# Attention and feed-forward on one Trainium2 core: when token loads, transposes and scores are issued

## The chip, the cores and the metric

The kernel runs on one core of a Trainium2 chip. Times are device microseconds (us). A run of one core has one time; I quote medians and say how many runs they are of. A profile shows one execution: its span goes from the first to the last instruction, and the time of that execution lies about 2 us above it. PE is TensorE, DVE VectorE, ACT ScalarE, POOL GpSimd and SP SyncE. PE multiplies; ACT and DVE empty its PSUM banks; POOL scales softmax rows, reorders tokens and issues the loads that cast to bf16; SP issues the DMA transposes and the output stores, in its program order.

## The reference, cut to what matters

```python
def _attn_ref(x, state):            # x (8, 8, 512, 64), state (8, 8, 32, 64)
    scale = 1.0 / np.sqrt(D)
    a = softmax(scale * x @ state.T)        # tokens read from the state
    xread = a @ state
    a2 = softmax(scale * state @ x.T)       # the state reads from the tokens
    sread = a2 @ x
    return np.concatenate([xread, sread], axis=2)

def _moe_ref(x, w1, w2, w3, w_out):         # 4352 rows of 512, d_ff 768
    h = np.maximum(np.maximum(x @ w1, x @ w2), x @ w3)
    return h @ w_out
```

(The softmax lines are abridged.) For each of eight batches the kernel folds `state @ w` into small matrices M, so that the up-projections of a batch are `M.T @ a.T`. They need the attention matrix transposed (`aT`); the scores need the tokens transposed (`xT`).

## The kernel before: the parts that matter

The program is written as strings of units, worked off in order. An opening handles batches 0 to 2, then one PERIOD string runs per batch and LAST ends it.

```python
PERIOD = """
u u u L u u S u S X o o u u P o o m M m u R u o o u m M m u u u u u u o u o
"""
...
    def load_x(b):                              # L: POOL issues the load, with a cast
        x_sb[b] = xlp.tile([128, H, J, D], BF16, tag="x", name="x")
        nc.gpsimd.dma_start(out=x_sb[b]..., in_=x[b]...)
...
            elif what == "S":
                scores(nb, sc.pop(0), "g")      # exp on ACT, sum on DVE, product a on POOL
            elif what == "P":
                if nb + 1 < B:
                    permute_x(nb + 1, None, "g")    # POOL: xn <- x
                    x_crossbar(nb + 1)              # SP: DMA transpose xT <- xn
            elif what == "L":
                if nb + 1 < B:
                    load_x(nb + 1)
            elif what == "X":
                a_crossbar(nb)                      # SP: DMA transpose aT <- a
```

In period t, `nb` is t + 2: that batch is scored, while the up-projections (`u`) of batch t + 1 and the output rows (`o`) of batch t run. The last rows of all:

```python
        if last and j == J - 1:
            half = d_model // 2
            for k in range(2):
                o = res.tile([128, half], F32, name=f"oh{k}")
                f = slice(k * half, k * half + half)
                copy("av"[k], o, po[:, f])          # ACT, then DVE, out of one bank
                (nc.scalar, nc.sync)[k].dma_start(out=rows[j][:, f], in_=o)
```

The softmax here doesn't subtract the row's maximum and nothing guards it: scores larger than these inputs give would overflow.

Of the kernel before, what the change touches and what calls it, by code (L numbers as in the profile page):

```python
# [8 lines left out]
F32 = mybir.dt.float32  # L9
# [16 lines left out]


OPENING = """
id, idle 9, sel, idle 9, pm 0 0 a, lx 1, pm 0 1 v, pm 1 0 v, lw 0 1, xT 0 0 a, lw 2 4,
pm 1 1 v, xT 0 1 a, lw 1 2, S 0 0 g, S 0 1 g, xT 1 0 a, xT 1 1 v, M 0 0 aa, M 1 0 av,  # L30
R 0, lw 4 6, S 1 1 g, lx 2, S 1 0 g, aT 0 0 a, idle 7, aT 0 1 a, M 0 3 aa, M 0 2 aa,
M 1 2 va, R 1, u 0 0 0, u 0 3 0, M 0 1 va, u 0 0 1, u 0 3 1, u 0 2 0, aT 1 - v, M 1 3 aa,
u 0 1 0, u 0 3 2, u 0 0 2, lx 3, u 0 1 1, M 0 5 aa, M 0 4 va, u 1 2 0, u 0 2 1, lo,
pm 2 - g, u 1 0 0, u 1 2 1, pm 3 - g, M 2 5 av, M 1 5 av, u 0 1 2, u 0 5 0, xb 3,
u 0 4 0, u 0 2 2, u 1 3 0, xT 2 0 a, u 0 5 1, u 0 5 2, M 1 4 aa, M 1 1 aa, u 0 4 1,
xT 2 1 v, u 1 2 2, u 1 0 1, u 0 4 2, S 2 0 g, u 1 3 1, u 1 1 0, u 1 5 0, S 2 1 g,
u 1 4 0, o 0 0 0 v, o 0 0 1 a, o 0 1 0 a, u 1 0 2, o 0 1 1 a, u 1 5 1, M 2 2 aa, ab 2,
M 2 3 aa, M 2 0 av, o 0 2 0 a, u 1 4 1, o 0 2 1 a, u 1 3 2, M 2 4 aa, M 2 1 aa, u 1 5 2,
u 1 1 1, R 2, o 0 3 0 v, o 0 3 1 a, u 1 1 2, u 1 4 2
"""  # L40


PERIOD = """
u u u L u u S u S X o o u u P o o m M m u R u o o u m M m u u u u u u o u o
"""
LAST = """
u u M M u u P u u u L S u R o S u u M X u u o M u u u M u u o M u o o o o o
"""


# [1 line left out]
def kernel(  # L52
# [14 lines left out]
    nc = tc.nc  # L67

    B, H, S, D = x.shape
    _, _, Ns, _ = state.shape  # L70
    HD = H * D
    SP = S + Ns
    d_model, d_ff = moe_w1.shape
    assert HD == d_model and D == 64 and Ns == 32 and H == 8 and S == 512
    J = S // 128
    HP = H // 2
    MT = d_ff // 128
# [6 lines left out]
    res = ctx.enter_context(tc.tile_pool(name="res", bufs=1))  # L84
# [9 lines left out]
    def bank(shape, dt, name):  # L94
        return psum.tile(shape, dt, tag="bank", name=name)
# [3 lines left out]
    def copy(eng, o, i):  # L99
        if eng == "a":  # L100
            nc.scalar.copy(out=o, in_=i)  # L101
        else:
            ENG[eng].tensor_copy(out=o, in_=i)  # L103

    def mm(out_ap, lhsT, rhs, start, stop, pos=(0, 0)):
        nc.tensor.matmul(out_ap, lhsT, rhs, start=start, stop=stop, tile_position=pos)  # L106

    def tr(out_ap, in_ap):
# [9 lines left out]
        out=st32.rearrange("p n d -> p (n d)"),  # L118
        in_=state.rearrange("b h (q n) d -> (b h q) (n d)", q=2))
# [3 lines left out]
                      in_=x[0].rearrange("h (p j) d -> p h (j d)", j=J))  # L123
# [12 lines left out]
    wout = res.tile([128, MT, d_model], BF16, name="wout")  # L136
# [14 lines left out]
    def load_x(b):  # L151
        x_sb[b] = xlp.tile([128, H, J, D], BF16, tag="x", name="x")
        nc.gpsimd.dma_start(
            out=x_sb[b].rearrange("p h j d -> p h (j d)"),
            in_=x[b].rearrange("h (p j) d -> p h (j d)", j=J))
# [23 lines left out]
    def m_unit(b, m, engs):  # L179
        pm = [bank([128, 512], F32, "pm") for _ in range(2)]  # L180
        for hp in range(HP):
            for par in range(2):
                r0 = par * 64
                mm(pm[par][hp * 32:(hp + 1) * 32, 0:384],
                   sbd[r0:r0 + 64, b, hp, par, :],
                   W[r0:r0 + 64, :, hp, m * 128:(m + 1) * 128],
                   True, True, pos=(r0, hp * 32))
        for par in range(2):
            copy(engs[par], M_sb[:, b, m, par].rearrange("p i f -> p (i f)"), pm[par][:, 0:384])


    tiles = {}
# [21 lines left out]
    def permute_x(b, h, eng):  # L214
        j = slice(0, J) if h is None else slice(2 * h, 2 * h + 2)
        i = x_sb[b][:, :, j] if b else x32[:, :, j]
        copy(eng, x_nat(b)[:, j], i.rearrange("p h j d -> p j h d"))

    def x_crossbar(b):
        nc.sync.dma_start_transpose(  # L220
            out=xT(b).rearrange("p j hp t -> p (j hp) t"),
            in_=x_nat(b).rearrange("p j h d -> p (j h d)"))
# [27 lines left out]
    def a_crossbar(b):  # L250
        nc.sync.dma_start_transpose(
            out=aT(b).rearrange("p j a t -> p (j a) t"),
            in_=a_of(b).rearrange("p j a hp n -> p (j a hp n)"))
# [32 lines left out]
    def up(g, m, i):  # L286

        nn = S if g < B else ST
        ht = tile_of("ht", g, htp, [128, MT, S])
        pw = bank([128, S], F32, "pw")  # L290
        if g < B:
            for par in range(2):
                mm(pw, M_sb[:, g, m, par, i, :], aT(g)[:, :, par, :], par == 0, par == 1)
        else:
            for hp in range(HP):
                mm(pw[:, :nn], W[:, i, hp, m * 128:(m + 1) * 128], AT[:, hp, :],
                   hp == 0, hp == HP - 1)
        if i == 0:
            t = tiles["t", g, m] = tmpp.tile([128, S], BF16, tag="t0", name="t0")
            nc.scalar.copy(out=t[:, :nn], in_=pw[:, :nn])  # L300
        elif i == 1:
            t0 = tiles["t", g, m]
            t = tiles["t", g, m] = tmpp.tile([128, S], BF16, tag="t1", name="t1")
            nc.vector.tensor_max(t[:, :nn], t0[:, :nn], pw[:, :nn])  # L304
        else:
            nc.vector.tensor_max(ht[:, m, :nn], tiles["t", g, m][:, :nn], pw[:, :nn])  # L306

    def out_half(g, j, h, eng):
        last = g == ORDER[-1]
        if h == 0:  # L310
            tiles["po"] = bank([128, d_model], F32, "po")
        po = tiles["po"]
        for kt in range(3 * h, 3 * h + 3):
            mm(po, tiles["ht", g][:, kt, j * 128:(j + 1) * 128], wout[:, kt, :],
               kt == 0, kt == MT - 1)
        if h == 0:
            return
        rows = out[g * SP:g * SP + S, :].rearrange("(p j) f -> j p f", j=J) if g < B else None
        if last and j == J - 1:
            half = d_model // 2  # L320
            for k in range(2):
                o = res.tile([128, half], F32, name=f"oh{k}")
                f = slice(k * half, k * half + half)
                copy("av"[k], o, po[:, f])
                (nc.scalar, nc.sync)[k].dma_start(out=rows[j][:, f], in_=o)
            return
        if j % 2 == 0:
            tiles["o"] = op.tile([128, 2, d_model], F32, tag="o", name="o")
        o = tiles["o"]
        copy(eng, o[:, j % 2, :], po)  # L330
        if last:
            nc.sync.dma_start(out=rows[j], in_=o[:, j % 2, :])
        elif g < B:
            if j % 2 == 1:
                nc.sync.dma_start(out=rows[j - 1:j + 1].rearrange("j p f -> p j f"), in_=o)
        else:
            for q in range(4):
                bb = 4 * j + q
                nc.sync.dma_start(out=out[bb * SP + S:(bb + 1) * SP, :],
                                  in_=o[q * 32:(q + 1) * 32, j % 2, :])  # L340
# [46 lines left out]
    for t in range(1, B):  # L387
        p, g = ORDER[t], ORDER[t + 1]
        nb = t + 2
        us = [(g, m, i) for m in range(MT) for i in range(3)]  # L390
        os = [(p, j, h) for j in range(J if p < B else ST // 128) for h in range(2)]
        sc = [0, 1]
        for what in (PERIOD if g != ORDER[-1] else LAST).split():
            if what == "u":
                up(*us.pop(0))
            elif what == "o":
                if os:
                    out_half(*os.pop(0), "a")
            elif what in ("M", "m"):
                if m_q:  # L400
                    m_unit(*m_q.pop(0), "aa" if what == "M" else "av")
            elif nb >= B:
                continue
            elif what == "S":
                scores(nb, sc.pop(0), "g")
            elif what == "P":
                if nb + 1 < B:
                    permute_x(nb + 1, None, "g")
                    x_crossbar(nb + 1)
            elif what == "L":  # L410
                if nb + 1 < B:
                    load_x(nb + 1)
            elif what == "R":
                state_reads(nb)
            elif what == "X":
                a_crossbar(nb)
    for j in range(J):
        for h in range(2):
            out_half(ORDER[-1], j, h, "a")
# [29 lines left out]
```

## Time and profile before

| | before |
|---|---|
| first timed runs | 170.55 us median of 3 (167.83 to 172.34) |
| the profiled execution | 165.97 us, span 163.9 us |
| PE busy | 151.4 us, 92% of the span |
| next busiest | DVE 68%, ACT 57% |
| PE idle after 17 us and before its end | 5.5 us in four holes |

PE sets the time, and the holes in its work are what can be gained; the prediction shows both. What it describes in words is the order in two queues. These are lines of the order of work in the kernel before, first of POOL's queue, then of SP's (start, length, engine, line, operation):

```profile
71.89 1.04 POOL L246 TENSOR_TENSOR a<-e,rden 128x512 bf16<-128x512 bf16 x1 [0.46 <-DVE rden L245]
72.88 1.89 POOL L103 COPY xn<-x 128x2048 bf16<-128x2048 bf16 x1
74.71 0.94 POOL L153 DMA_DIRECT2D x<-in_x_dram  x1
...
72.96 1.24 SPq L251 DMA_TRANSPOSE aT<-a  x1
74.79 2.52 SPq L220 DMA_TRANSPOSE xT<-xn  x1
```

POOL reorders one batch's tokens as soon as its softmax products are done, and then at once issues the next load (74.71). The end of the same reordering releases the token transpose on SP (74.79). The two start within 0.1 us of each other, in every period that has a load.

### The profile page before, as it was taken

Reading aid. Unit: us, or ns where it says so; the run is one execution under the profiler, and the core shown is the slowest. Engines: PE = TensorE matmul, PEld = TensorE weight load, DVE = VectorE, ACT = ScalarE, POOL = GpSimd, SP = SyncE. Lnnn points to the kernel's source line nnn. Section 1 sums busy time; section 2 is a strip of 40 time slices with the busy share of each in tenths; the row PEclk is TensorE's granted clock in tenths of the full one; section 3 lists DMA queues with packets and bytes.
Section 4 is the critical chain, followed back from the end, with each engine's and each line's share of the span. In section 5 each row is a group of like instructions: output and inputs, shape, how many; then the busy total and the mean of one; then the engine's idle time right before and its main releaser. Section 6 shows DMA issues by size and latency. Waiting matters only on the chain. (4 is left out here: it accounts for less than half of the span.)

```text
span 163.9 us, 3537 instructions
## 1 busy us (share of the span) xinstructions
PE 151.4 (92%) x1389; PEld 74.7 (46%) x1389; DVE 112.0 (68%) x203; ACT 93.5 (57%) x184; POOL 44.6 (27%) x48
## 2 busy tenths in 40 slices
PE   7979999999929999799969999999999999999990
PEld 2455544554405444344424444454544476844430
DVE  3349999886836888578957797789778942558601
ACT  3688869776515665556545764576656534344340
POOL 8838944425000830074004600450050000000000
PEclk9999999999999999999999999999999999999999
DMA  5999999943990099907991899156306031130263
GB/s 166 286 185 196 187 198 201 159 101 79 154 194 24 4 161 112 285 18 119 116 287 57 87 173 285 42 117 203 134 0 192 0 132 65 63 128 0 68 192 130
DMA packets 35457, 21.73 MB, mean 133 GB/s; under 512 B 20592, under 2 KB 32880, under 8 KB 35440
## 3 DMA queue, kind: packets, MB, share of 16 engines
q1 hardware_dynamic: 20896, 14.55, 36.9%
q0 software_dynamic: 14400, 6.82, 35.9%
q8 instruction: 11, 0.18, 0.5%
q10 hardware_dynamic: 144, 0.13, 0.2%
q14 instruction: 6, 0.05, 0.1%
HBM read 15.20 MB, written 8.91 MB: 147 GB/s over the span
## 5 line engine op out<-in xcount | busy, mean ns | idle before, releaser
L106 PE MATMUL pw<-aT,M_sb 128*128 128x512 bf16 x288 | 72.2, 380 | 3.0 <-DMA aT<-a 3.0
L106 PE MATMUL po<-wout,ht 128*128 128x512 bf16 x204 | 50.4, 379 | 0.0
L304 DVE TENSOR_TENSOR t<-t,pw 128x512 bf16<-128x512 bf16 (+1 forms) x54 | 35.0, 650 | 20.7 <-ACT t L300 11.1
L106 PEld LDWEIGHTS <-M_sb 128*128 128x128 bf16 x288 | 25.7, 98 | 35.2 <-issue 4.8
L300 ACT CAST t<-pw 128x512 bf16<-128x512 f32 (+1 forms) x54 | 30.4, 572 | 18.8 <-PE pw L106 17.8
L306 DVE TENSOR_TENSOR ht<-t,pw 128x512 bf16<-128x512 bf16 (+1 forms) x54 | 34.9, 650 | 6.1 <-PE pw L106 3.4
L101 ACT COPY o<-po 128x512 f32<-128x512 f32 x33 | 19.3, 586 | 34.4 <-PE po L106 34.2
L246 POOL TENSOR_TENSOR a<-e,rden 128x512 bf16<-128x512 bf16 x16 | 16.6, 1041 | 69.3 <-ACT e L238 45.7
L101 ACT CAST M_sb<-pm 128x384 bf16<-128x384 f32 x69 | 28.4, 498 | 2.0 <-PE pm L106 1.3
L106 PEld LDWEIGHTS <-ht 128*128 128x128 bf16 x204 | 19.5, 98 | 21.8 <-issue 0.3
L103 DVE CAST M_sb<-pm 128x384 bf16<-128x384 f32 x27 | 14.0, 551 | 3.5 <-PE pm L106 3.5
L242 DVE TENSOR_REDUCE den<-e 128x16 f32<-128x512 bf16 x16 | 10.8, 672 | 3.5 <-ACT e L238 3.3
L103 POOL COPY xn<-x 128x2048 bf16<-128x2048 bf16 x6 | 11.4, 1892 | 4.8 <-DMA x<-in_x_dram 4.8
L238 ACT ACTIVATE e<-ps 128x512 bf16<-128x512 f32 x16 | 9.5, 599 | 5.3 <-PE ps L106 5.0
L106 PE MATMUL pm<-W,sbd 64*32 64x384 bf16 x384 | 11.8, 327 | 0.0
L106 PE MATMUL ps<-sbd,xT 128*128 128x64 bf16 x128 | 6.2, 193 | 4.1 <-DMA xT<-xn 2.6
L144 POOL DMA_DIRECT2D W<-in_moe_w_dram x12 | 9.0, 773 | 2.7 <-DMA x<-in_x_dram 2.7
L106 PE MATMUL pz<-zeros 128*128 128x512 bf16 x25 | 8.2, 486 | 1.2 <-DVE zeros L125 1.2
L106 PEld LDWEIGHTS <-xT 128*128 128x128 bf16 x128 | 5.3, 98 | 8.2 <-DMA xT<-xn 4.0
L106 PE MATMUL pw<-AT,W 128*128 128x256 bf16 x72 | 8.7, 273 | 0.0
L106 PEld LDWEIGHTS <-W 128*128 128x128 bf16 x72 | 7.0, 98 | 1.9
L279 DVE RECIPROCAL rd<-pr 128x128 f32<-128x128 f32 x8 | 7.6, 955 | 0.0
(38 smaller groups left out, 66.1 us busy)
## 6 DMA issues: line engine op xcount, KB each, us to landing
out_dram<-o SPq DMA_DIRECT2D x14, 512.0 KB, 4.1
x<-in_x_dram POOLq DMA_DIRECT2D x7, 512.0 KB, 9.3
W<-in_moe_w_dram POOLq DMA_DIRECT2D x6, 256.0 KB, 7.9
x<-in_x_dram SPq DMA_DIRECT2D x1, 1024.0 KB, 6.3
W<-in_moe_w_dram POOLq DMA_DIRECT2D x6, 128.0 KB, 8.4
wout<-in_moe_w_out_dram POOLq DMA_DIRECT2D x1, 768.0 KB, 12.2
out_dram<-o SPq DMA_DIRECT2D x3, 256.0 KB, 2.0
st<-in_state_dram SPq DMA_DIRECT2D x1, 512.0 KB, 3.4
```

The costliest lines, as they stand in the source:

```text
L101: nc.scalar.copy(out=o, in_=i)
L103: ENG[eng].tensor_copy(out=o, in_=i)
L106: nc.tensor.matmul(out_ap, lhsT, rhs, start=start, stop=stop, tile_position=pos)
L144: nc.gpsimd.dma_start(out=W[:, i, :, c], in_=w_v[i][:, :, c])
L238: nc.scalar.activation(out=e.rearrange("p r n -> p (r n)"), in_=ps.rearrange("p j a hp n -> p (j a hp n)"), func=AF.Exp, scale=scale)
L242: nc.vector.reduce_sum(out=den, in_=e, axis=AX.X)
L246: ENG[eng].tensor_mul(out=a_of(b)[:, 2 * h:2 * h + 2].rearrange("p j a hp n -> p (j a hp) n"), in0=e, in1=rden.unsqueeze(2).to_broadcast(( ...
L279: nc.vector.reciprocal(out=rd, in_=pd.rearrange("p (hp n) -> p hp n", hp=HP))
L300: nc.scalar.copy(out=t[:, :nn], in_=pw[:, :nn])
L304: nc.vector.tensor_max(t[:, :nn], t0[:, :nn], pw[:, :nn])
L306: nc.vector.tensor_max(ht[:, m, :nn], tiles["t", g, m][:, :nn], pw[:, :nn])
```

## The change

Its intent: no DMA transpose should be waited for. The tokens of a batch are reordered and transposed at the head of a period, before that period's scores; loads go two batches ahead so that they have arrived by then; the attention of batch 2, which meets the end of the opening, is transposed by PE; and the last rows go into two half-width PSUM banks, so that ACT and DVE can copy independently. The diff, its opening cut to the lines that count:

```diff
 OPENING = """
-id, idle 9, sel, idle 9, pm 0 0 a, lx 1, pm 0 1 v, pm 1 0 v, lw 0 1, xT 0 0 a, lw 2 4,
+id, idle 9, sel, idle 9, pm 0 0 a, pm 0 1 v, lx 1, xT 0 0 v, lw 2 4, pm 1 1 v, pm 1 0 v,
+xT 0 1 a, idle 8, lw 1 2, lw 0 1, S 0 0 g, S 0 1 g, xT 1 1 a, xT 1 0 a, R 0, lw 4 6,
  [...]  (loads: lx 3, lx 2 instead of lx 2, lx 3; lx 4 added after pm 2)
-u 1 4 0, o 0 0 0 v, o 0 0 1 a, o 0 1 0 a, u 1 0 2, o 0 1 1 a, u 1 5 1, M 2 2 aa, ab 2,
+o 0 1 1 a, o 0 2 0 v, o 0 2 1 a, M 2 0 aa, M 2 4 aa, aT 2 - v, u 1 4 0, u 1 0 2, u 1 5 2,
 PERIOD = """
-u u u L u u S u S X o o u u P o o m M m u R u o o u m M m u u u u u u o u o
+u u u P L S S o o u M M m o u u o u u u o u u o X u M m m R u o u u u o u u
 LAST = """      [...]  (the same units in another order)
     def out_half(g, j, h, eng):
+        if last and j == J - 1:
+            half = d_model // 2
+            f = slice(h * half, h * half + half)
+            po = bank([128, half], F32, "po")
+            for kt in range(MT):
+                mm(po, ht[:, kt, j * 128:(j + 1) * 128], wout[:, kt, f], kt == 0, kt == MT - 1)
+            o = res.tile([128, half], F32, name=f"oh{h}")
+            copy("av"[h], o, po)
+            (nc.scalar, nc.sync)[h].dma_start(out=rows[j][:, f], in_=o)
+            return
  [...]
             elif what == "L":
-                if nb + 1 < B:
-                    load_x(nb + 1)
+                if nb + 2 < B:
+                    load_x(nb + 2)
```

More of the change, by code (lines that the diff above doesn't have):

```diff
@@ L28 @@
 OPENING = """
-id, idle 9, sel, idle 9, pm 0 0 a, lx 1, pm 0 1 v, pm 1 0 v, lw 0 1, xT 0 0 a, lw 2 4,
-pm 1 1 v, xT 0 1 a, lw 1 2, S 0 0 g, S 0 1 g, xT 1 0 a, xT 1 1 v, M 0 0 aa, M 1 0 av,
-R 0, lw 4 6, S 1 1 g, lx 2, S 1 0 g, aT 0 0 a, idle 7, aT 0 1 a, M 0 3 aa, M 0 2 aa,
-M 1 2 va, R 1, u 0 0 0, u 0 3 0, M 0 1 va, u 0 0 1, u 0 3 1, u 0 2 0, aT 1 - v, M 1 3 aa,
-u 0 1 0, u 0 3 2, u 0 0 2, lx 3, u 0 1 1, M 0 5 aa, M 0 4 va, u 1 2 0, u 0 2 1, lo,
-pm 2 - g, u 1 0 0, u 1 2 1, pm 3 - g, M 2 5 av, M 1 5 av, u 0 1 2, u 0 5 0, xb 3,
-u 0 4 0, u 0 2 2, u 1 3 0, xT 2 0 a, u 0 5 1, u 0 5 2, M 1 4 aa, M 1 1 aa, u 0 4 1,
-xT 2 1 v, u 1 2 2, u 1 0 1, u 0 4 2, S 2 0 g, u 1 3 1, u 1 1 0, u 1 5 0, S 2 1 g,
-u 1 4 0, o 0 0 0 v, o 0 0 1 a, o 0 1 0 a, u 1 0 2, o 0 1 1 a, u 1 5 1, M 2 2 aa, ab 2,
-M 2 3 aa, M 2 0 av, o 0 2 0 a, u 1 4 1, o 0 2 1 a, u 1 3 2, M 2 4 aa, M 2 1 aa, u 1 5 2,
-u 1 1 1, R 2, o 0 3 0 v, o 0 3 1 a, u 1 1 2, u 1 4 2
+id, idle 9, sel, idle 9, pm 0 0 a, pm 0 1 v, lx 1, xT 0 0 v, lw 2 4, pm 1 1 v, pm 1 0 v,
+xT 0 1 a, idle 8, lw 1 2, lw 0 1, S 0 0 g, S 0 1 g, xT 1 1 a, xT 1 0 a, R 0, lw 4 6,
+S 1 1 g, aT 0 0 a, M 0 2 va, aT 0 1 v, S 1 0 g, M 0 3 aa, M 1 3 av, M 1 2 aa, M 2 1 vv,
+u 0 3 0, u 0 3 1, M 0 1 aa, u 0 2 0, M 1 1 va, aT 1 - v, u 0 2 1, M 0 0 aa, R 1, u 0 1 0,
+lx 3, u 1 1 0, u 0 2 2, u 0 0 0, u 1 1 1, M 0 5 aa, M 0 4 aa, lx 2, u 0 1 1, u 0 3 2, lo,
+u 1 3 0, u 0 0 1, u 0 5 0, M 1 0 va, pm 2 - g, u 1 3 1, u 1 1 2, u 0 4 0, M 2 2 aa,
+u 1 3 2, lx 4, u 0 5 1, pm 3 - g, u 1 0 0, M 2 5 aa, M 1 5 aa, xb 3, u 0 1 2, u 0 5 2,
+u 1 2 0, xT 2 1 v, u 0 4 1, u 0 0 2, u 1 5 0, u 0 4 2, xT 2 0 a, u 1 0 1, S 2 1 g,
+o 0 0 0 v, M 1 4 aa, M 2 3 aa, o 0 0 1 v, u 1 2 1, o 0 1 0 v, S 2 0 g, u 1 5 1, u 1 2 2,
+o 0 1 1 a, o 0 2 0 v, o 0 2 1 a, M 2 0 aa, M 2 4 aa, aT 2 - v, u 1 4 0, u 1 0 2, u 1 5 2,
+o 0 3 0 v, o 0 3 1 a, u 1 4 1, u 1 4 2, R 2
 """
 PERIOD = """
-u u u L u u S u S X o o u u P o o m M m u R u o o u m M m u u u u u u o u o
+u u u P L S S o o u M M m o u u o u u u o u u o X u M m m R u o u u u o u u
 """
 LAST = """
-u u M M u u P u u u L S u R o S u u M X u u o M u u u M u u o M u o o o o o
+u u u u u u M M u u u S u o u o u u M u u R u u M o u o S M L o M P o o X o
 """
@@ L309, in out_half @@
         last = g == ORDER[-1]
+        rows = out[g * SP:g * SP + S, :].rearrange("(p j) f -> j p f", j=J) if g < B else None
+        ht = tiles["ht", g]
+        if last and j == J - 1:
[8 more added lines that the diff above has]
+            return
         if h == 0:
@@ L313, in out_half @@
         for kt in range(3 * h, 3 * h + 3):
-            mm(po, tiles["ht", g][:, kt, j * 128:(j + 1) * 128], wout[:, kt, :],
-               kt == 0, kt == MT - 1)
+            mm(po, ht[:, kt, j * 128:(j + 1) * 128], wout[:, kt, :], kt == 0, kt == MT - 1)
         if h == 0:
-            return
-        rows = out[g * SP:g * SP + S, :].rearrange("(p j) f -> j p f", j=J) if g < B else None
-        if last and j == J - 1:
-            half = d_model // 2
-            for k in range(2):
-                o = res.tile([128, half], F32, name=f"oh{k}")
-                f = slice(k * half, k * half + half)
-                copy("av"[k], o, po[:, f])
-                (nc.scalar, nc.sync)[k].dma_start(out=rows[j][:, f], in_=o)
             return
```

## The prediction

> **What bounds the kernel now.** I read the page's busy table first, then the list of waits, then the order of work on TensorE (PE), then the queues of SP and POOL. The busy table:
>
> ```profile
> PE 151.4 (92%) x1389; PEld 74.7 (46%) x1389; DVE 112.0 (68%) x203; ACT 93.5 (57%) x184; POOL 44.6 (27%) x48
> ```
>
> PE is first by a wide margin. Cut into stretches (start and end in us, length, then the busy time of each engine, clock, DMA share, GB/s), the trace shows that it is full except in a few holes:
>
> ```profile
> 17.00:46.08 29.08, 29.08 (x312) 13.43 (x307) 24.46 (x44) 21.72 (x46) 11.65 (x11) 1.00 1.11 153
> 46.08:49.04 2.96, 0.00 (x2) 0.01 (x1) 0.89 (x2) 0.00 (x0) 0.00 (x0) 1.00 0.88 203
> ...
> 68.08:85.41 17.33, 15.94 (x148) 7.35 (x148) 12.99 (x24) 9.92 (x20) 4.79 (x4) 1.00 0.88 138
> 85.41:101.59 16.18, 15.94 (x149) 7.38 (x149) 11.85 (x22) 9.92 (x20) 4.79 (x4) 1.00 0.93 146
> 101.59:117.37 15.78, 15.78 (x149) 7.47 (x150) 12.66 (x24) 9.57 (x20) 3.91 (x3) 1.00 0.44 130
> ```
>
> The last three are one period of the steady state each (scores to scores). The undisturbed one is 15.78 us; the others are longer only by a hole. DVE is busy 12.66 of 15.78 us there, so it isn't the bound. PE's own waits name the holes:
>
> ```profile
> PE pw L106 <- DMA aT<-a: 3.0, 1, 3.0
> PE ps L106 <- DMA xT<-xn: 2.6, 3, 1.4
> ```
>
> So 3.0 us at 46.08 us, where the up-projections of batch 2 wait for its attention matrix from the DMA transpose, and 0.94, 1.39 and 0.23 us at 67.1, 84.0 and 101.4 us, where scores wait for transposed tokens. In all 5.5 us of PE idle after 17 us. Why the transposes are late is in the issues, seen in the windows around them (name, queue, count, us to landing):
>
> ```profile
> x<-in_x_dram POOLq DMA_DIRECT2D x1, 512.0 KB, 11.3
> xT<-xn SPq DMA_TRANSPOSE x1, 10.6
> ...
> xT<-xn SPq DMA_TRANSPOSE x1, 3.6
> ```
>
> The first two are the pair issued at 74.7 us, the last was issued at 108.66 us, when no load ran. The same transpose takes 3.6 us alone and 9.4 to 10.6 us beside a token load. In this order POOL copies the tokens of one batch (which releases their transpose) and at once issues the next load, so the two always meet. Batch 2's attention transpose had the same fate: issued at 39.38 us, 0.9 us after a load and 0.45 us after an output store, it took 9.6 us; the later ones, issued about 1.8 us before a load, took 3.1 to 4.9 us, and 3.0 with no load.
>
> The end is a chain:
>
> ```profile
> 158.69 1.03 PE L106 MATMUL po<-wout,ht 128*128 128x512 bf16 x4
> ...
> 159.76 0.37 ACT L101 COPY oh<-po 128x256 f32<-128x256 f32 x1 [0.67 <-PE po L106]
> ...
> 160.16 0.42 DVE L103 COPY oh<-po 128x256 f32<-128x256 f32 x1 [5.49 <-ACT oh L101]
> 160.61 0.33 SPq L325 DMA_DIRECT2D out_dram<-oh  x1
> ```
>
> ACT copies one half of the last rows, then DVE the other, and only then the last store goes (1.9 us to landing).
>
> **What the Trainium skill says.** "DMA: Bandwidth & Descriptors", section "Issuing engines are not separate DMA queues": transfers from SP, ACT and POOL end on the same 16 DMA engines and interleave. The trace agrees (3.6 against 9.4 to 10.6 us). "PSUM — Partial Sum Buffer", section "PSUM bank collisions raise a hardware error": two engines may not read the same bank and quadrant at once, so a dependency must keep them apart. The trace agrees: DVE's half waited for ACT's (from 159.74 to 160.16). "TensorE: Matmul & The Clock Gate", section "Part 4: PE-mode transpose": a 128x128 transpose shows about 275 ns in one kernel. Here one shows 219 ns, but they are pipelined: sixteen took 1.06 us, so a slot is about (1.06 - 0.17)/16 = 0.056 us; I use the slot. The same page, "What's actually happening": after an idle window of about 3.4 us the clock halves. The 2.96 us hole kept clock 1.00; a longer one in another run might not.
>
> **The change part by part.** A PE slot of 128x512 is 0.216 us (six output matmuls are 1.29 us in the chain).
>
> 1. Batch 2's attention goes through the array. It removes the 2.96 us hole. It adds eight transposes (8 x 0.056 = 0.45 us of PE) and one DVE copy of 0.68 us, where DVE has room (24.46 of 29.08 us in the opening). Net -2.5 us.
>
> 2. Period: the copy and the transpose of tokens stand at its head, loads go two batches ahead, both scores follow, the attention transpose comes 9.7 us in. PE work is unchanged: 18 up units x 0.431 + 8 halves x 0.647 + 6 M units x 0.205 + reads 0.81 + scores 0.46 = 15.44 us before and after. One M copy of 0.5 us moves from DVE to ACT, which is busy 9.6 of 15.78. When the token transpose now starts: POOL runs ahead of PE, so its copy follows the previous period's attention products, some 6 us into that period (scores at 1.3, exp, sum, reciprocal, two products of 1.04 each, as the row distances of before give); but SP takes its queue in order, so the transpose goes out only behind the previous period's last output store, about at the period's end. The load, issued at about 8 us, has had 7 us of its 9 by then. The transpose lands by some 6 us into its period and is wanted 1.3 us into the next: over 10 us to spare, where before it had none. That removes 0.94 + 1.39 + 0.23 = 2.56 us.
>
> 3. Opening order: one idle matmul more (0.22 us), other order of loads and units. The tokens of batch 1 arrive at about 10.1 us as before. Eight idle matmuls now put both scores at about 11.4 us. Then ACT's queue decides: two exps 1.2, two token copies 2.0, exp 0.6, attention copy 0.6, half an M unit 0.5, exp 0.6, M unit 1.0, which ends at about 18.3 us. The first up-projection starts then (before: 18.43 us), but by my count of slots it has 11.4 us of PE work behind it, not 12.0. So PE is 0.6 us behind at that point. Later ACT carries a burst of M copies and may starve PE for up to 1 us, or regain as much; I book 0. Sum +0.8 us with the idle matmul.
>
> 4. Last rows in two banks: twelve matmuls of half width for six, the same streaming time (256-wide ones run at about 0.109 us: 24 in 2.62 us). The first half is copied and stored 0.65 us before PE ends; DVE's copy starts at PE's end and not 0.40 us later. -0.4 us. The moved units of the last stretch meet a PE that was full there: 0.
>
> Sum: -2.5 - 2.56 + 0.8 - 0.4 = -4.7 us. I add +0.3 for rival A: span 163.9 - 4.4 = 159.5 us, and with the 2.07 us that the profiled execution had beyond its span (165.97), 161.6 us.
>
> The timed runs stood at 167.83, 170.55 and 172.34 us, 2 to 6 above that profiled run. PE work doesn't vary so; I take it that the holes do, as they end on transfers that compete. Then the changed kernel, without them, should lose part of this excess as well. I choose a little under half of it: 161.6 + 1.9 = 163.5 us.
>
> **The rivals.**
>
> A. The attention transpose takes over the wait. It now stands behind an output store of 512 KB, at about 7.4 us, while the next load goes out at about 7.7 to 8.6 us: nearly batch 2's case of before, with 9.6 us. It would land near 17 us, wanted at 15.44: a new hole of 1 to 2 us. For: the order of issue. Against: loads remain only for batches 5, 6 and 7, and the one for 6 should be held back by its predecessor, so it meets at most one or two of five. Cost 0 to 4 us; I book 0.3. If it came in full: 165 to 167 us.
>
> B. The opening is the bound: the batch 2 tokens are now loaded after batch 3's, POOL's copy ends at about 31.7 us by the old durations (7.7 to 8.4 us a load, 1.9 the copy), and PE wants them at about 32.7 us. For: 1 us of margin only. Against: before had 0.8 us and it held. Cost if it fails: 1 to 2 us, so 165 us.
>
> C. Banks: three M units in a row take six of eight PSUM banks, of which ACT empties five at 0.5 us. For: PE could catch up with the ring. Against: other units of 0.43 to 0.65 us lie between, and ACT had 6 us free per period. I expect at most 0.2 us per period, 1 us in all.
>
> D. The excess of the timed runs is constant and nothing of it is regained: 161.6 + 4.6 = 166.2 us, still just over 2% faster.
>
> **Range and chances.** Low: all of the excess goes, 160.5. High: D with some of A or C, 167. Faster by over 2% means under 167.1; that fails only if two rivals come together: 0.88. Within 2%: 0.11. Slower: 0.01, as nothing is added beyond 0.7 us of PE work.
>
> **What would show it.** Right: no PE wait on aT at the first up-projection of the second period; none on xT at scores; five token transposes at 3.6 to 6 us or landing well ahead; periods of 15.4 to 15.8 us; DVE's last copy starting at PE's end; span 158 to 161. Wrong: PE waits named aT in later periods (A), a wait on ACT or DVE copies of xT in the opening (B), PE idle on M_sb, t or o copies (C), a first up-projection later than 19.5 us, or timed runs as scattered as before.

## The result, and the profile after

| | before | after |
|---|---|---|
| median | 170.32 us of 4 (167.83 to 172.34) | 160.03 us of 4 (159.57 to 160.05) |
| ratio of fast runs | | 0.9465 (95%: 0.9353 to 0.9577) |
| profiled execution | 165.97 us, span 163.9 | 160.03 us, span 158.2 |

A ratio is the mean time of one kernel's fast runs over that of the other's in the same rounds, so it is not quite the ratio of the medians. The record calls a run slow when it is over 1.5% above the fastest of the same kernel, fast otherwise; the medians here are of all runs, slow ones too. The change makes the kernel 5% faster. I had predicted 163.5 us, so it gained more than that; the median lies 0.5 us under the low end of the range, 160.5. (By the ratio, 0.9465 x 170.55 = 161.4, it lies inside.) The scatter went too: 0.5 us between the four runs, against 4.5.

In the kernel after, PE's own waits are these, in full:

```profile
PE pz L106 <- DVE zeros L125: 1.2, 1, 1.2
PE pa L109 <- POOL a L246: 0.7, 2, 0.4
PE px L109 <- ACT xn L101: 0.7, 1, 0.7
PE pm L106 <- ACT M_sb L101: 0.4, 1, 0.4
```

All lie ahead of 18 us, in the start-up. No line names `xT` or `aT` by DMA. Cut into stretches at the scores (columns as in the prediction), the steady state has one length, 15.77 us, with a load (first line) and without one:

```profile
64.24:80.01 15.77, 15.67 (x148) 7.44 (x148) 12.63 (x24) 10.29 (x21) 4.76 (x4) 1.00 0.77 151
80.01:95.78 15.77, 15.66 (x148) 7.44 (x149) 12.62 (x24) 10.29 (x21) 3.87 (x3) 1.00 0.44 118
```

POOL's queue and SP's queue in one of these periods, from the order of work:

```profile
53.68 1.88 POOL L103 COPY xn<-x 128x2048 bf16<-128x2048 bf16 x1
55.51 0.94 POOL L153 DMA_DIRECT2D x<-in_x_dram  x1
...
54.35 0.34 SPq L338 DMA_DIRECT2D out_dram<-o  x1
54.78 1.45 SPq L251 DMA_TRANSPOSE aT<-a  x1
62.89 0.34 SPq L338 DMA_DIRECT2D out_dram<-o  x1
63.41 2.48 SPq L220 DMA_TRANSPOSE xT<-xn  x1
```

POOL does as before: copy, then load. But SP stands behind the period's last store (62.89), so the token transpose goes out 7.9 us after the load and not with it. The load and the transpose (name, queue, count, us to landing):

```profile
x<-in_x_dram POOLq DMA_DIRECT2D x1, 512.0 KB, 7.7
...
xT<-xn SPq DMA_TRANSPOSE x1, 4.4
```

The load was in at 63.21 us, just before the transpose went out; this transpose took 4.4 us instead of 9.4 to 10.6, and has the whole next period before its scores. The end:

```profile
154.16 0.37 ACT L101 COPY oh<-po 128x256 f32<-128x256 f32 x1
...
154.82 0.42 DVE L103 COPY oh<-po 128x256 f32<-128x256 f32 x1 [5.15 <-PE po L106]
155.27 0.33 SPq L321 DMA_DIRECT2D out_dram<-oh  x1
```

ACT started its copy 0.6 us before PE was done (its last group of output matmuls starts at 148.77 and takes 6.00, so 154.77), and DVE waited for PE, no longer for ACT.

Where the 5.7 us between the spans went, from three marks in both traces:

| stretch | before | after | difference |
|---|---|---|---|
| start to first up-projection of batch 2 | 49.04 | 47.16 | -1.9 |
| from there to PE's end | 110.70 | 107.61 | -3.1 |
| PE's end to the end | 4.20 | 3.46 | -0.7 |

This adds up to the traces, but the times fell by about 10 us (170.32 - 160.03), 4 more than the profiled executions. What was not visible in the single trace of before is the first question for the experiments.

### The profile page after: what moved, and what is told of

Its sections match the earlier page's. It is cut to its first block, busy times and chain, and to the rows that moved or that the text cites. A ratio compares the mean times of both kernels' runs of the same rounds, so it can differ in the third digit from the quotient of the medians.

```text
span 158.2 us, 3558 instructions
## 1 busy us (share of the span) xinstructions
PE 150.8 (95%) x1387; PEld 76.1 (48%) x1404; DVE 112.0 (71%) x200; ACT 94.8 (60%) x188; POOL 44.3 (28%) x48
## 4 chain that ended last, share of the span: by engine, by line
PE 88%; DMA 4%; ACT 2%; POOL 1%; issue 1%; DVE 1%; SPq 0%; POOLq 0%
PE pw L106 45%; PE po L106 28%; PE pm L106 6%; DMA x<-in_x_dram 4%; PE pr L106 4%; PE ps L106 2%; PE px L109 1%; POOL a L246 1%; PE pz L106 1%; PE pa L109 1%; ACT e L238 1%; ACT xn L101 1%; ACT M_sb L101 0%; DVE den L242 0%; DVE oh L103 0%
## 5 line engine op out<-in xcount | busy, mean ns | idle before, releaser
L106 PE MATMUL po<-wout,ht 128*128 128x512 bf16 (+1 forms) x194 | 51.1, 373 | 0.8
L106 PEld LDWEIGHTS <-M_sb 128*128 128x128 bf16 x288 | 26.9, 98 | 31.5 <-issue 1.0
L101 ACT CAST M_sb<-pm 128x384 bf16<-128x384 f32 x75 | 30.9, 504 | 1.3 <-PE pm L106 0.5
L101 ACT COPY o<-po 128x512 f32<-128x512 f32 x32 | 18.8, 586 | 18.6 <-PE po L106 16.1
L103 POOL COPY xn<-x 128x2048 bf16<-128x2048 bf16 x6 | 11.3, 1887 | 8.1 <-DMA x<-in_x_dram 8.1
L106 PE MATMUL pm<-W,sbd 64*32 64x384 bf16 x384 | 12.4, 327 | 0.5 <-ACT M_sb L101 0.4
L242 DVE TENSOR_REDUCE den<-e 128x16 f32<-128x512 bf16 x16 | 10.6, 661 | 2.0 <-ACT e L238 1.9
L238 ACT ACTIVATE e<-ps 128x512 bf16<-128x512 f32 x16 | 8.9, 598 | 4.6 <-PE ps L106 4.6
L103 DVE CAST M_sb<-pm 128x384 bf16<-128x384 f32 x21 | 10.6, 534 | 0.0
L106 PE MATMUL pw<-AT,W 128*128 128x256 bf16 x72 | 9.2, 273 | 0.1
L106 PEld LDWEIGHTS <-sbd 64*32 64x32 bf16 x384 | 4.3, 89 | 9.7 <-issue 9.1
L153 POOL DMA_DIRECT2D x<-in_x_dram x7 | 6.6, 942 | 0.1
## 6 DMA issues: line engine op xcount, KB each, us to landing
W<-in_moe_w_dram POOLq DMA_DIRECT2D x6, 128.0 KB, 10.9
```

The source lines that it names most:

```text
L101: nc.scalar.copy(out=o, in_=i)
L103: ENG[eng].tensor_copy(out=o, in_=i)
L106: nc.tensor.matmul(out_ap, lhsT, rhs, start=start, stop=stop, tile_position=pos)
L153: nc.gpsimd.dma_start(out=x_sb[b].rearrange("p h j d -> p h (j d)"), in_=x[b].rearrange("h (p j) d -> p h (j d)", j=J))
L238: nc.scalar.activation(out=e.rearrange("p r n -> p (r n)"), in_=ps.rearrange("p j a hp n -> p (j a hp n)"), func=AF.Exp, scale=scale)
L242: nc.vector.reduce_sum(out=den, in_=e, axis=AX.X)
```

## The experiments

Three theories stood for those 4 us, under the names that the expectations use: H, the lengths of the holes vary between executions; C, the excess is constant and outside the holes; K, a hole lets the TensorE clock fall, and the clock then costs extra. For the trace itself two questions were open: what of the change does the work, and whether the meeting of load and transpose is the cause of the holes. All twelve runs were correct. They went in three jobs of four, each on one chip; "before" in a row, or the yardstick, is the kernel before, timed in the rounds of the same job. Its fast runs have a mean of 167.43 us (5 of 11) in the first job, 168.31 (4 of 11) in the second and 168.14 (4 of 7) in the third; the ratios rest on these, the medians given beside them on all. The edits are cut to the units or lines that differ.

### The kernel before, again: five rounds and three looks

No edit. The five rounds:

> The kernel before, unchanged, to see where its timed runs lose the 4 us that its profiled run (165.97) did not show. Theory H (holes vary): the executions differ in the length of their waits on transposes; spans scatter from about 164 to 170 with the times, clock stays 1.00, and a traced execution longer than 166 has PE holes before the first pw<-aT and before ps<-xT of more than 5.5 us in sum. Theory C (constant excess): spans stay at 164 within 0.5 us and the excess lies outside the span. Theory K (clock): the long executions have a mean clock clearly under 1.00, because one hole lets the TensorE clock fall.

The looks:

> The kernel before again, one look, to catch the trace of an execution longer than 168 us. H: what it is longer than the 163.9 us span by is found again as longer PE holes before ps<-xT and pw<-aT (5.6 us in the first trace). C: the holes are 5.6 us again and the rest lies elsewhere.

> A second look at the kernel before, with the same expectations: under H the extra span equals the extra PE holes before ps<-xT and pw<-aT; under C the holes stay at 5.6 us.

> A third look at the kernel before, with the same expectations: under H the extra span equals the extra PE holes before ps<-xT and pw<-aT; under C the holes stay at 5.6 us.

Measured: b0_again 166.30 us median of 6 (165.44 to 168.95); the looks 166.58, 167.14 and 169.11 us. With the first trace that makes five traced executions. Holes are PE's idle times before the first up-projection of batch 2 and before the scores:

| execution | span | holes: batch 2, scores | time at half clock | span - holes - half of the time at half clock |
|---|---|---|---|---|
| first trace | 163.9 | 2.96 + 2.56 | 0 | 158.4 |
| b0_look1 | 164.7 | 2.80 + 3.23 | 0 | 158.7 |
| b0_look2 | 165.3 | 3.21 + 3.38 | 0 | 158.7 |
| b0_again | 165.4 | 2.62 + 4.15 | 0 | 158.6 |
| b0_look3 | 167.0 | 2.82 + 3.80 | 3.41 | 158.7 |

(In b0_look1 one of the score holes, 1.11 us, is put down by the profile to a DVE instruction; it stands before scores like the others, so I count it. The clock also falls at the very end of the later four, after the last matmul; that costs nothing and isn't counted.) What is left is constant within 0.3 us, so H holds for the first four: their holes go from 5.5 to 6.8 us. The first trace, on which I had built, was the shortest of the five. The 167.0 us execution needs K as well. Its stretches around the hole of batch 2 (columns as before; the third number from the right is the granted clock):

```profile
46.36:49.18 2.82, 0.01 (x1) 0.00 (x0) 0.90 (x2) 0.00 (x0) 0.00 (x0) 1.00 1.03 208
49.18:51.00 1.82, 1.82 (x6) 0.75 (x7) 0.20 (x1) 0.59 (x1) 0.00 (x0) 0.62 0.24 90
51.00:53.00 2.00, 2.00 (x6) 0.67 (x5) 1.17 (x2) 0.52 (x1) 0.00 (x0) 0.50 0.00 0
53.00:55.00 2.00, 2.00 (x24) 1.15 (x23) 1.42 (x3) 1.26 (x3) 0.00 (x0) 0.99 0.00 0
```

After a hole of 2.82 us the clock is 1.00 for a moment, then 0.50 until 53.0 us, then back. The records give the half clock as 3.41 us long. The ten up-projection matmuls in it show it as well; in the order of work of b0_look3 and of b0_look2:

```profile
49.18 4.02 PE L106 MATMUL pw<-aT,M_sb 128*128 128x512 bf16 x10 [2.82 <-DMA aT<-a]
...
49.55 2.33 PE L106 MATMUL pw<-aT,M_sb 128*128 128x512 bf16 x10 [3.21 <-DMA aT<-a]
```

The first took 4.02 us, the second, after a longer hole but at full clock, 2.33: 1.7 us lost. "TensorE: Matmul & The Clock Gate", section "What's actually happening", says that the clock falls after an idle window of about 3.4 us and that the windows run freely. Two things agree: the half clock lasted 3.41 us, and much the same hole cost nothing in four executions and 1.7 us in one. One doesn't: the hole that was followed by half clock is shorter than a window (2.82 us as shown, 2.98 from the end of the last slot), so no window can have been idle throughout. What decides whether the clock falls is not shown here. So C falls, and H and K each have a part.

No execution above 169.1 us was traced, though the kernel before had timed runs up to 172.34. But the record lists span and mean granted clock of each run in the jobs. Of 38 executions of the kernel before, with spans of 163.4 to 169.6 us, eleven were 168.3 us or longer (slow runs by the record, all of them), and their mean clock was 0.956 to 0.980. Half clock in all of the 4.2 us after the last matmul would take only 0.013 off the mean, so in these eleven the clock was down elsewhere too. All 26 executions with the changed period and opening had 0.996 or more; the four of b_period, described below, had 0.987 to 1.000. So the clock has a part in the longest executions of before. Where in them it fell is not recorded, and the link isn't strict: three runs with spans of 163.4 to 164.0 us had 0.983 to 0.986. What also isn't settled: as the yardstick of its job the same kernel had a median of 168.88 us of 11, against 166.30 of 6 under test (ratio of fast runs 0.9933, 0.9862 to 1.0003, so unclear), for which I have no cause. Idle matmuls put into the hole of batch 2 would test the clock's share; that wasn't run.

### Only batch 2's attention through the array (b_aT2)

```diff
-M 2 2 aa, ab 2,
+M 2 2 aa, aT 2 - v,
```

> The kernel before with only batch 2's attention transposed by the array instead of by DMA. By the hole seen in the trace (2.96, plus 0.16 because the last matmul before a hole is shown with 0.38 us instead of its slot of 0.216) less eight transposes (0.45): span about 161.2 us. Under H the first up-projection of batch 2 has no wait left, the time falls by 2.5 us or more (some of the excess was in this hole) and the rest of the scatter remains, as the xT holes remain. Under C exactly 2.7 us.

Measured: 162.98 us median of 4 (162.36 to 163.40), before 168.88, ratio 0.9731 (0.9660 to 0.9802); span 161.4. The span is as expected, but in part by luck: in this trace the first up-projection started 0.46 us later than in the first trace (18.89 against 18.43), and PE's waits on xT were two of 2.1 us in all instead of three of 2.56. The time fell by more than the 2.7 us of theory C: by fast runs 4.5 us under the yardstick and 3.4 under b0_again. The scatter shrank to 1 us, though the scores still wait. That fits the hole of batch 2 as one place where the excess arises; it does not prove that it was the clock.

### Only the new period and the load distance (b_period)

```diff
-pm 2 - g, u 1 0 0,
+pm 2 - g, lx 4, u 1 0 0,
-u u u L u u S u S X o o u u P o o m M m u R u o o u m M m u u u u u u o u o
+u u u P L S S o o u M M m o u u o u u u o u u o X u M m m R u o u u u o u u
-                    load_x(nb + 1)
+                    load_x(nb + 2)
```

> The kernel before with only the new period order and loads two ahead (batch 4 is then loaded in the opening); batch 2's attention still goes by DMA. If the order is what frees the scores: no PE wait on xT at all, periods of 15.8 us, token transposes landing in under 7 us. The batch 2 transpose now no longer follows right after a load (that of batch 4 is issued about 8 us earlier), so if the load was what delayed it, its hole of 2.96 us shrinks to under 1 us by itself; if the output store ahead of it was the cause, the hole stays at about 3 us. Span 158 to 161 us; under H the scatter of times goes too.

Measured: 160.17 us median of 4 (159.58 to 160.69), before 168.88, ratio 0.9565 (0.9496 to 0.9635); span 157.8. This part alone gives what the whole change gives (160.03 in its own job). PE's waits in its trace end with the start-up ones; there is none on xT, and none on aT though batch 2 still goes by DMA. Its store and its transpose, issued at 39.03 and 39.49 us, almost as in the kernel before (38.93 and 39.38):

```profile
out_dram<-o SPq DMA_DIRECT2D x1, 512.0 KB, 2.9
aT<-a SPq DMA_TRANSPOSE x1, 3.7
```

3.7 us instead of 9.6, behind the same store. In this kernel the load of batch 4 went out at 28.10 us instead of 38.49, and the next only at 40.43, 0.94 us after the transpose and not 0.89 us ahead of it. So it was the load ahead and not the store that had delayed batch 2's transpose, and a load that followed 0.94 us behind did it no harm.

### The changed kernel with batch 2 by DMA again (a_ab2)

```diff
-M 2 4 aa, aT 2 - v,
+M 2 4 aa, ab 2,
```

> The changed kernel with batch 2's attention by DMA again. If the array is needed beside the new period: a PE hole at the first up-projection of batch 2 of 2 us or more and 1.5 us or more longer. If the new load order alone already frees the transpose: no hole, and 0.45 us shorter by the eight transposes saved, 159.5 us.

Measured: 159.92 us median of 4 (159.55 to 161.24), before 170.03, ratio 0.9522 (0.9411 to 0.9633); span 157.7, no wait on aT. The unchanged kernel in the same job:

> The changed kernel unchanged, as the yardstick for the other runs of this set: 159.6 to 160.1 us, span 157.8 to 158.3.

Measured: a_again 159.80 us median of 6 (159.54 to 159.91), ratio 0.9493 (0.9438 to 0.9548); span 158.0. The medians are the same within the scatter. Beside the new period the array for batch 2 buys nothing in the median; its 0.45 us of PE shows at most in the traced spans (157.7 against 158.0). One of the four runs of a_ab2 took 161.24 us at a clock of 1.000, 1.3 us above any run of a_again; it was not traced, so whether the array buys steadiness stays open.

### The changed kernel with the old period (a_oldperiod1, a_oldperiod2)

Both take the period string of before. a_oldperiod1 also loads one batch ahead as before (`lx 4` leaves the opening); a_oldperiod2 keeps two.

> The changed kernel with the period order and the load distance of before (batch 4 not loaded in the opening). If the period is worth the three xT holes: about 3 us longer in the trace (161 us of span), PE waits on xT at scores of 0.2 to 1.4 us again, token transposes at 9 to 11 us. Under H the timed runs scatter again by 1 us or more and are up to 4 us longer than the changed kernel's; under C they are 3 us longer and steady.

> The changed kernel with the period order of before but loads still two ahead: the distance alone. In the trace of before POOL never waits for a token load in the steady state, and the next load is issued right behind the copy whichever batch it brings. So if the meeting of load and transpose is the cause, the distance alone does nothing: token transposes land at 9 to 11 us, PE waits on xT of 0.2 to 2.3 us stay, 164 to 166 us as with the old period and loads one ahead (165.86). If the load's lateness was the cause: no holes, 160 us.

Measured: a_oldperiod1 165.86 us median of 4 (163.81 to 166.49), before 168.88, ratio 0.9832 (0.9709 to 0.9955); a_oldperiod2 164.66 us of 4 (163.80 to 166.04), before 168.97, ratio 0.9774 (0.9660 to 0.9888). Spans 162.0 and 162.4. PE waits for xT again, in a_oldperiod1 and in a_oldperiod2:

```profile
PE ps L106 <- DMA xT<-xn: 3.0, 2, 2.3
...
PE ps L106 <- DMA xT<-xn: 2.9, 2, 2.3
```

By fast runs the two are alike: means of 164.62 us (two runs; the other two are slow) and 164.79 (four). The distance alone does next to nothing. In a_oldperiod2 a token transpose issued beside a load took 10.9 us, while one issued at 91.96 us, when no load was left to issue, took 3.7: the meeting, not the lateness of the load, makes the holes. I take it that two batches ahead is needed only so that the order can be changed: with the copy at the head of a period its tokens must have been loaded in the period before. The new order with loads one ahead wasn't run. And the runs scatter by 2.7 and 2.2 us, though neither trace has a hole at batch 2, so the scatter of before does not all come from that hole. The mean clock of these runs goes down to 0.975, so it falls here too; those runs weren't traced.

The trace of a_oldperiod2 holds one thing more. Its opening is that of the changed kernel, and there PE waited for POOL's copy of batch 2's tokens, which is rival B of the prediction:

```profile
33.28 0.62 PE L109 MATMUL px<-ident,xn 128*128 128x128 bf16 x8 [0.91 <-POOL xn L103]
```

### The tail (a_tail1)

The changed kernel with the `out_half` of before:

```diff
-            po = bank([128, half], F32, "po")
-            for kt in range(MT):
-                mm(po, ht[:, kt, j * 128:(j + 1) * 128], wout[:, kt, f], kt == 0, kt == MT - 1)
  [...]  (the six full-width matmuls into one bank are back)
+            for k in range(2):
+                o = res.tile([128, half], F32, name=f"oh{k}")
+                f = slice(k * half, k * half + half)
+                copy("av"[k], o, po[:, f])
```

> The changed kernel with its last rows in one bank again, as before. If the two banks are worth what the chain at the end of before says, DVE's last copy starts 0.40 us after PE's end again and the time is 0.4 us longer (160.4 us); if the last store's landing hides it, no change.

Measured: 160.16 us median of 6 (160.02 to 160.90) against 159.80 for a_again, so 0.4 us; means of six 160.29 and 159.78. In its trace DVE waits for ACT again:

```profile
154.84 0.37 ACT L101 COPY oh<-po 128x256 f32<-128x256 f32 x1 [0.67 <-PE po L106]
...
155.25 0.42 DVE L103 COPY oh<-po 128x256 f32<-128x256 f32 x1 [5.54 <-ACT oh L101]
```

DVE starts 0.41 us after ACT did, and not at PE's end. The two banks are worth that.

### Fewer idle matmuls ahead of the first scores (a_idle4)

```diff
-xT 0 1 a, idle 8, lw 1 2,
+xT 0 1 a, idle 4, lw 1 2,
```

> The changed kernel with 4 instead of 8 idle matmuls ahead of the first scores. If these idle matmuls delay the chain that feeds the first up-projection (scores at 11.41 us although ACT has their tokens at 10.9), first up-projection 0.4 to 0.6 us earlier and the time 0.4 to 0.6 us shorter (159.5). If ACT's queue or the weights decide, or the clock falls without them, the same or longer.

Measured: 159.44 us median of 6 (159.42 to 159.97), ratio 0.9479 (0.9423 to 0.9536), against 159.80 of a_again; means 159.55 and 159.78. The first up-projection starts at 17.59 us, against 18.04 in the trace of the result and 17.84 in that of a_again:

```profile
17.30 0.35 PE L106 MATMUL pm<-W,sbd 64*32 64x384 bf16 x8 [0.43 <-DMA W<-in_moe_w_dram]
17.59 1.04 PE L106 MATMUL pw<-aT,M_sb 128*128 128x512 bf16 x4
```

The row ahead of it now waits for weights, so the next limit there is a load. This version beats both kernels, by 0.2 to 0.4 us over the changed one, well under 1%; four of its six runs lie below the lowest of a_again, one among them and one above them.

## Why the prediction was right or wrong

- **The bound and the holes: right.** PE without holes runs a period in 15.77 us; I had taken 15.78 from the undisturbed one.
- **Step 1, batch 2 through the array: right in its arithmetic, wrong as a cause.** The hole went, and alone the array takes the span to 161.4 (161.2 expected, in part by luck as said above). But in the whole change the new load order would have removed the hole anyway (b_period, a_ab2). I had seen that the transpose followed a load, and had not asked what the other part would do to that load.
- **Step 2, the period: right in its mechanism.** Loads at 8 us into the period, transposes at its end, landing in 4.4 to 6.7 us: as worked out. Undersized: the three holes were worth 3.1 us and not 2.56, because an idle entry starts at the shown end of the last matmul (0.379 us long) and not at the end of its slot (0.216). Each hole costs 0.16 us more than its entry, 0.48 in all; that is an account from the trace, not an experiment. The sum of 15.44 us of PE work per period also falls 0.3 short of the 15.77 measured; only differences were used, so nothing came of it.
- **Step 3, the opening: right.** Scores at 11.41 us (11.4 expected), first up-projection at 18.04 (18.3), batch 2's at 47.16, 1.9 us earlier with step 1 (1.7 expected).
- **Step 4, the tail: right.** -0.4 us by a_tail1. The two traces differ by 0.7 us there; the rest, 0.4, lies after the last store was issued (3.3 us to the end before, 3.0 after). That store lands after 1.9 us in both, so I have no cause for it.
- **Rival A came once and was covered.** One attention transpose, issued at 70.57 us behind a store and beside a load, took 7.4 us and landed at 77.97, some 0.7 us before it was wanted (80.01 - 1.29 = 78.72). Booked 0.3 us, cost 0. **Rival B** was closer than I thought: I gave 1 us of margin, but POOL's copy ended at 32.48 us, not 31.7, and PE took the tokens at 32.54. In a_oldperiod2, with the same opening, it cost 0.91 us. **Rival C** did not show: no PE wait on banks after 18 us. **Rival D**, the constant excess, is refuted by the result itself and by the five traces of before.
- **The step that failed** is "I choose a little under half of it", with what it took over from the profile: I left 1.9 us of the excess of the timed runs in the changed kernel. Nothing of it stayed: its timed runs and its profiled run agree at 160.0. The reason I gave, that holes end on competing transfers and vary, holds (5.5 to 6.8 us), and the clock adds 1.7 us when it falls. I had named it only in passing, for a hole longer than 2.96 us; it fell after one of 2.82. The error is a term of the sum: of the 3.5 us between 163.5 and 160.03, 1.9 are this excess, 1.3 the span (159.5 against 158.2: the holes' 0.48, the 0.3 for rival A and the rest), and 0.2 the time beyond the span (1.83 instead of 2.07).

## What to carry to other kernels

The slow transfers here were those that met a load: look at what was issued just ahead of a slow transfer (here up to about 3 us), and let an in-order queue keep the two apart, before moving work to another engine. If timed runs scatter while engine work doesn't, look for waits that vary and for the granted clock; one trace is one draw. Here the change that removed the waits took away the whole excess of the timed runs over the traced one. Try the parts of a change alone: two of them may remove the same hole.

## What the Trainium skill lacked or had wrong

- "DMA: Bandwidth & Descriptors", section "Issuing engines are not separate DMA queues", says that transfers interleave, but not at what price: in the periods of the eight traces with the old order a DMA transpose of 128x2048 bf16 took 3.6 to 3.7 us from issue to landing with no load about, and 8.8 to 11.3 us when issued 0.1 to 0.5 us behind a casting load of a batch's tokens (512 KB). At 2.8 us behind a load it took 6.3 us (the changed kernel) and 9.4 (a_ab2).
- "TensorE: Matmul & The Clock Gate", section "What's actually happening", gives an idle window of about 3.4 us. In b0_look3 a hole shown as 2.82 us was followed by 3.41 us at half clock (1.7 us lost), in b0_look2 one of 3.21 us was not. That a hole shorter than a window can cost a whole one, and not in each execution, is missing in that section.
- "Perfetto Trace Analysis", section "Identifying the Most-Contended Engine", warns that pipelined matmuls make PE's busy time a bad measure of the distance from its peak, but not that idle entries come out too short: here a 128x512 matmul is shown with 0.379 us and takes a slot of 0.216, so each hole is 0.16 us longer than shown.
